# Attention with a gated squared-ReLU branch on one core: key, value and output-weight loads split, and two output rows moved to other buffers

## The chip, the cores and the metric

The kernel runs on one core of one Trainium2 chip, as one launch. The core has five engines that each run their own list of instructions in order: TensorE (PE) for matmuls, VectorE (DVE), ScalarE (ACT), GpSimd (POOL) and SyncE (SP), which here only issues transfers. They meet through semaphores. The metric is the device time of one execution in microseconds; the time before is the median of five.

## The reference

A layer norm of x (2048 rows of 512) feeds two branches: attention over a given cache of keys and values (32 heads, 2048 keys, head size 128) and a dense branch with a squared ReLU. The output is x plus their product, the dense branch passed through silu.

```
xn = _layernorm(x)
q  = (xn @ wq) per head                       # wq: 512 x 4096
p  = softmax(q @ k_cache^T * 128 ** -0.5)
s  = concat over heads of (p @ v_cache) @ wo  # wo: 4096 x 512
h  = xn @ w1 + b1                             # w1: 512 x 1792
g  = silu(relu(h) ** 2 @ w2 + b2)
return x + s * g
```

All inputs and the output are bfloat16.

## The kernel before

The 2048 rows are cut into NQB = 4 blocks of 512 query rows. A block goes through all 32 heads, so there are NG = 128 heads of work, numbered g = 0 to 127. The 2048 keys of a head are taken 256 at a time: NPR = 8 steps a head, 1024 steps (`pi`) in all. In a step `gen_scores` (lines 658 to 691) makes two matmuls of 512 columns into PSUM (`psA`, two halves in turn), and one ACTIVATE on ACT takes the exp of 128 x 1024 scores into one of NPT = 8 buffers of `pT`. Two steps later (LAG = 2) the probabilities meet the values.

That second product has two forms. In form A (`gen_pv`, line 952) the probabilities are the stationary operand, and a column of ones beside the values gives the softmax's denominator: 64 matmuls of 129 columns a head. DVE then copies the result to `o_un`, divides it, and a DMA transpose on SP's queue brings it into `oT`. In form B (`gen_pv_b`, line 713) the values are stationary: 16 matmuls of 512 columns a head, and the result comes out already transposed (`o_col`). The denominator must then be made apart: POOL adds the two halves of a step's probabilities into `h_sum` (`part_add`, line 745) and DVE reduces that into `d_part` (`part_half`, 753), or DVE does both alone (`den_part`, 732). `den_sum`, `den_write`, `den_read`, `den_total`, `den_recip`, `den_spread` and `den_scale` (lines 764 to 810) bring the sums together by way of a small DRAM tensor, `d_scr`, spread the reciprocals into `r_all`, and POOL scales `o_col` into `oT`. A `pT` buffer is free again only when the value matmuls and the denominator's reads of it are done; the exp eight steps later waits for that.

Which form a head takes, and in which order everything stands on each engine, is settled while the program is built. The class `_Sched` keeps a clock for each engine, from the rough costs in `_cost` (line 60) and, for DMAs on SP, the pairs (issue, landing) in `_ISSUE` (line 97). `choose` takes form B unless the first or last three heads are at hand or `owed`, the planned backlog of DVE, is 9000 ns or more. Denominator work waits in lists (`quiet`, `pool_quiet`, `sync_quiet`) and is put between other instructions where that clock has room (`fill_dve`, `fill_pool`, `fill_sync`, lines 892 to 946). So an edit that changes an entry of `_ISSUE`, or adds an instruction to SP, can change the order on all engines.

Beside attention TensorE has jobs (`job_proj`, `job_h`, `job_o2`, `job_wo`, lines 1048 to 1186) that `fill_one` puts between the steps: the projection of the queries two heads ahead, the dense branch, and the output product in groups of eight heads. The output product's parts are summed in `acc`; `acc_gate` (line 1194) multiplies `acc` by the gate on DVE, `acc_add` (1201) adds x on POOL, and the last part is multiplied by the gate into `tmp_t`, added to `acc` and written out. Row tiles, 128 rows each, are numbered jt = 0 to 15. Their results stand in `out_t`, which has two buffers used in turn, but for the very last, jt = 15, which goes to `x_t`.

Transfers into SBUF are almost all issued by SP, in order. `kT` and `v_sb` have NSL = 3 slots, one a head. In step k = 0 of head g the loop issues `fill_wq(g + 3)` and `fill_k(g + 2)` (a DMA transpose of the head's 2048 x 128 keys), and in step 1 `fill_v(g + 2)` (512 KB). A key load waits for the last score of the head that used the slot, a value load for its last value product. The output weights come in four loads of 1 MB at steps 60, 84, 108 and 132. Between these stand `den_write` and `den_read`, the `oT` transposes, and in the opening the loads of w1 and w2.

Of the kernel before, what the change touches and what calls it, by code (L numbers as in the profile page):

```python
# [10 lines left out]
P = 128  # L11
# [73 lines left out]
def _uses_port(name, fn):  # L85
# [3 lines left out]
    if name == "DVE":  # L89
        if f in (_tt, _stt):  # L90
            return _in_sbuf(k["in0"]) and _in_sbuf(k["in1"])
        if f in (_ts, _copy):
# [1 line left out]
    return False  # L94


_ISSUE = {"kT": (2450, 4900), "oT": (1230, 3400), "xnT": (1230, 3400), "v_sb": (450, 4750),
          "wo_all": (1700, 7200), "w1_sb": (600, 5000), "w2_sb": (700, 5000), "d_scr": (530, 2200),
          "d_quad": (1230, 4200)}


# [199 lines left out]
def bass_recurrent_scan__mha_block_cached__dense_activation_squared_relu__prompt_kernel(  # L301
# [14 lines left out]
    _, H, Sk, Dh = A_k_cache.shape  # L316
# [3 lines left out]
    NQB = Sq // QB  # L320
    TPB = QB // P
    NDC = D // P
    NKT = Sk // P
    NPR = NKT // 2
# [6 lines left out]
    HC = 8  # L331
    NCH = H // HC
    CH = [[(m * HC, (m + 1) * HC) for m in range(NCH)] for _ in range(NQB - 1)]
    CH.append([(0, HC), (HC, 2 * HC), (2 * HC, H)])
    LAG = 2
    ROOM = 800
    LATE = 150
    LATE_EVICT = 250
# [6 lines left out]
    S = _Sched()  # L345
# [4 lines left out]
    SP = S.eng("SP")  # L350
# [9 lines left out]
    xnT = sb("xnT", [P, NDC, 2 * QB], BF16)  # L360
    w1_sb = sb("w1_sb", [P, NDC, F], BF16)
    w2_sb = sb("w2_sb", [P, NFC, D], BF16)
    wo_all = sb("wo_all", [P, H, D], BF16)
    h2T = sb("h2T", [P, NFC, QB], BF16)
    g_all = sb("g_all", [P, TPB, D], BF16)
    oT = sb("oT", [P, NOT, QB], BF16)
    acc = sb("acc", [P, TPB, D], F32)
    kT = sb("kT", [P, NSL, Sk], BF16)
    v_sb = sb("v_sb", [P, NSL, NKT, VW], BF16)
# [14 lines left out]
    d_scr = nc.dram_tensor("d_scr", [2, 32, 4 * NBK], F32, kind="Internal").ap()  # L384
# [25 lines left out]
    def bankF(i):  # L410
        return psF[:, i * 512:(i + 1) * 512]
# [4 lines left out]
    sl_k = [S.slot(f"k{i}") for i in range(NSL)]  # L416
    sl_v = [S.slot(f"v{i}") for i in range(NSL)]
# [9 lines left out]
    sl_wo = [S.slot(f"wo{i}") for i in range(NCH)]  # L427
# [94 lines left out]
    t_kT0 = [None, None]  # L522
# [88 lines left out]
    t_kfill = [None] * NG  # L611
    t_vfill = [None] * NG
    t_wqfill = [None] * NG
    t_S_last = [None] * NG
    t_PV_last = [None] * NG
# [8 lines left out]
    t_wodone = {}  # L624
    wo_view = A_wo.rearrange("(h p) d -> p h d", p=P)

    def fill_k(g):
        if g >= NG:
            return
        h, i, prev = g % H, g % NSL, g - NSL  # L630
        t_kfill[g] = S.emit_dma(SP, partial(_dmaT, out=kT[:, i, :], in_=A_k_cache[0, h, :, :]),
                                sl_k[i], deps=[t_S_last[prev] if prev >= 0 else t_kT0[1]])

    def fill_v(g, eng=SP):
        if g >= NG:
            return
        h, i, prev = g % H, g % NSL, g - NSL
        t_vfill[g] = S.emit_dma(
            eng, partial(_dma, out=v_sb[:, i, :, 0:Dh],
                        in_=A_v_cache[0, h].rearrange("(t p) d -> p t d", p=P)), sl_v[i],  # L640
            deps=[t_PV_last[prev] if prev >= 0 else None])

    def fill_wq(g, eng=SP):
        if g >= NG:
# [4 lines left out]
                        in_=A_wq[:, h * Dh:(h + 1) * Dh].rearrange("(c p) e -> p c e", p=P)),  # L649
            sl_wq[i], deps=[t_proj[prev] if prev >= 0 else None])  # L650

    def load_wo(i):
        tok_wo[i] = S.emit_dma(
            SP, partial(_dma, out=wo_all[:, i * HC:(i + 1) * HC, :],
                        in_=wo_view[:, i * HC:(i + 1) * HC, :]), sl_wo[i])


    def gen_scores(pi):
# [161 lines left out]
    def calm(due, fn):  # L820
        quiet.append((due, fn if isinstance(fn, partial) else partial(fn)))
# [130 lines left out]
    def gen_pv(pi):  # L952
# [40 lines left out]
        if last:  # L993
            t_PV_last[g] = t
            m = a_no[g]
            for b in range(2):
# [3 lines left out]
                    deps=[t_bank[b], t_norm[m - 1] if m else None], late=LATE_EVICT)  # L1000
            calm(pi + LAG + 3, partial(norm_recip, g))
            pool_quiet.append(partial(norm_scale, g))
# [42 lines left out]
    def at(step, fn):  # L1045
        events.setdefault(step, []).append(fn)
# [86 lines left out]
    def job_wo(j, m, qt, c0=0, c1=D):  # L1133
        jt = j * TPB + qt
        h0, h1 = CH[j][m]
        nh = h1 - h0
        last = m == len(CH[j]) - 1
        box = [None]

        def mm(n, bank):  # L1140
            g = j * H + h0 + n
            assert tok_oT[g] is not None
            place, free = (bankF(bank), t_bankF[bank]) if isinstance(bank, int) else bank
            box[0] = E(PE, partial(_mm, out=place[:, 0:c1 - c0],
                                   lhsT=oT[:, g % NOT, qt * P:(qt + 1) * P],
                                   rhs=wo_all[:, h0 + n, c0:c1], start=(n == 0),
                                   stop=(n == nh - 1)),
                       deps=[tok_wo[(h0 + n) // HC], tok_oT[g], free], inc=(n == nh - 1))

        def evac(bank, step):  # L1150
            if qt == TPB - 1:
                for h in range(h0, h1):
                    t_wodone[j * H + h] = box[0]
            place = (bankF(bank) if isinstance(bank, int) else bank[0])[:, 0:c1 - c0]
            if m == 0:
                t_acc[qt] = t = E(DV, partial(_copy, out=acc[:, qt, :], in_=place),
                                  deps=[box[0], t_fin.get(jt - TPB)])
            elif not last:
                t_acc[qt] = t = E(DV, partial(_tt, out=acc[:, qt, :], in0=place,
                                              in1=acc[:, qt, :], op=ALU.add),  # L1160
                                  deps=[box[0], t_acc[qt]])
            if m == len(CH[j]) - 2:
                calm(step + 16, partial(acc_gate, j, qt))
                pool_quiet.append(partial(acc_add, j, qt))
            if last:
                s = jt % 2
                assert all(x in t_g for x in t_o2j)
                t = E(DV, partial(_stt, out=tmp_t[:, s, c0:c1], in0=place, scalar=0.5,
                                  in1=g_all[:, jt % TPB, c0:c1], op0=ALU.mult,
                                  op1=ALU.mult),  # L1170
                      deps=[box[0], t_g[jt], t_tmp[s], t_zrd[s]])
                end = jt == NQB * TPB - 1
                row = (x_t if end else out_t)[:, s, c0:c1]
                eng = GP if j == NQB - 1 and qt in (0, 2) else DV
                t_fin[jt] = t_tmp[s] = E(
                    eng, partial(_tt, out=row, in0=tmp_t[:, s, c0:c1],
                                 in1=acc[:, qt, c0:c1], op=ALU.add),
                    deps=[t, t_u[jt], None if end else t_outdma[s]])
                eng, sl = (SP, sl_fin) if j == NQB - 1 else (GP, sl_out)
                dma = S.emit_dma(  # L1180
                    eng, partial(_dma, out=out[0, jt * P:(jt + 1) * P, c0:c1],
                                 in_=row), sl[s], deps=[t_fin[jt]])
                if c1 == D:
                    t_outdma[s] = dma
            return t
        return nh, mm, evac
# [23 lines left out]
    for j in range(NQB):  # L1210
        b = 30 + j * (SPB - 6)
        for c in range(NFC):
            k = b + (SPB * 9 // 256) * c
            jobs.append((k, max(k - 130, 4), job_h(j, c), (None, j)))
        for qt in range(TPB):
            k = b + (SPB * 9 // 256) * NFC + (SPB * 28 // 256) * qt
# [113 lines left out]
    for i in range(NFC // 2):  # L1330
        at(40 + 2 * i, partial(load_w2, i))
    for i in range(NCH):
        at(60 + 24 * i, partial(load_wo, i))
    for j in range(NQB):
        if j + 1 < NQB:
            for i in range(TPB):
# [69 lines left out]
    end = NPAIR  # L1406
    backfill[0] = fill_dve
    for pi in range(NPAIR):
        g, k = divmod(pi, NPR)
        if k == 0 and g > 0:  # L1410
            m = len(b_heads)
            choose(g, FIRST_B <= g < NG - 3 and owed(pi) < OWED and (m < NOC or m - NOC in t_dr))
            if is_b(g):
                plan_b(g)
        if pi >= NPR:
            gen_scores(pi)
        credit = 1.0 if pi < NPR else min(credit + left[0] / max(end - pi, 1), 8.0)
        n = 0
        most = 0 if pi < NPR else 3 if k == 2 else 2
        while n < most:  # L1420
            late = any(isinstance(p, int) and NPR * p <= pi + 12
                       for p in [cur_proj[0]] + [x[3] for x in jobs[:4]])
            if not (credit >= 1.0 or late):
                break
            if k == 1 and cur[0] is not None and cur[0][1] == cur[0][0][0] - 1:
                break
            if not fill_one(pi) and not (not jobs and tail_one(pi)):
                break
            credit = max(credit - 1.0, 0.0)
            left[0] -= 1  # L1430
            n += 1
        if pi >= NPR:
            gen_pv(pi - LAG)
        if k == 0:
            fill_wq(g + 3)
            fill_k(g + 2)
        if k == LAG - 1:
            fill_v(g + 2)
        pending.extend(events.pop(pi, []))
        if k >= 2:  # L1440
            for fn in [pending.pop(0) for _ in range(min(2, len(pending)))]:
                fn()
        fill_all(ROOM)
    for pi in range(NPAIR - LAG, NPAIR):
        gen_pv(pi)
    while quiet or pool_quiet or sync_quiet:
        n = len(quiet) + len(pool_quiet) + len(sync_quiet)
        fill_all(ROOM, flush=True)
        assert len(quiet) + len(pool_quiet) + len(sync_quiet) < n
# [42 lines left out]
```

## Time and profile before

| | us |
|---|---|
| median of 5 runs (1220.05 to 1220.60) | 1220.38 |
| the profiled execution, its own time | 1220.05 |
| its span, first instruction to last | 1218.3 |
| ACT busy: 1025 exps of 128 x 1024, 1.024 each | 1036.7 of 1088.5 |
| POOL busy: 764 additions into `h_sum`, 1.163 each | 867.0 of 1067.4 |
| DVE busy: 764 reductions of `h_sum`, 0.686 each | 506.3 of 1077.5 |
| key transposes from the second head on: 127, median to landing | 4.6 |
| value loads of 512 KB: 127, median to landing | 4.4 |

Busy time is the union of an engine's instructions. A matmul of 512 columns is shown with 0.379 us, but matmuls overlap in the array, so that their starts lie closer together. PE is the matmuls, PEld the weight loads that run beside them. A line of the timeline or of the groups names the engine, the helper's line, the operation, what it writes and reads, the shapes and the count; in square brackets stands how long the engine was idle before it, and who ended that.

### The profile page before, as it was taken

To read this page: it belongs to the slowest core of one execution; us is meant where nothing else is said; L and a number is where in the kernel's file an instruction comes from. 1 tells how busy PE (TensorE), PEld (TensorE's weight loads), DVE (VectorE), ACT (ScalarE), POOL (GpSimd) and SP (SyncE) were. 2 spreads that over 40 slices of the span, in tenths; PEclk is the share of its full clock that TensorE was granted. 3 is DMA by queue.
4 is the path that set the end of the run, shared out by engine and by line. 5 is a ranking of instruction groups with operands and counts; after the bars stand their busy time and mean duration, and the time that the engine had idled before them with its cause. 6 is when DMAs were issued, how large, how long until landed. Compare 5 with 4: busy or idle time off the path is not lost.

```text
span 1218.3 us, 19228 instructions
## 1 busy us (share of the span) xinstructions
PE 1206.2 (99%) x6386; PEld 588.4 (48%) x6509; DVE 1077.5 (88%) x1820; ACT 1088.5 (89%) x1157; POOL 1067.4 (88%) x978
## 2 busy tenths in 40 slices
PE   9999999999999999999999999999999999999998
PEld 7544444445454454444554444444444544444455
DVE  4798999898989888999999989898999899889983
ACT  7898999998988989999899899998989999989994
POOL 1799999998978989999888899999989789899981
PEclk9999999999999999999999999999999999999999
DMA  9998886667777776766687677766776687667651
GB/s 226 201 228 173 178 172 126 132 135 140 138 153 147 138 137 129 141 136 127 138 146 166 133 136 142 140 127 130 142 141 132 132 157 135 129 131 146 130 119 31
DMA packets 655492, 174.83 MB, mean 144 GB/s; under 512 B 642176, under 2 KB 654208, under 8 KB 655392
## 3 DMA queue, kind: packets, MB, share of 16 engines
q1 hardware_dynamic: 653296, 169.52, 70.1%
q0 software_dynamic: 1424, 3.81, 1.1%
q8 instruction: 52, 0.85, 0.3%
q14 instruction: 48, 0.39, 0.1%
q10 hardware_dynamic: 672, 0.26, 0.1%
HBM read 100.27 MB, written 3.01 MB: 85 GB/s over the span
## 4 chain that ended last, share of the span: by engine, by line
PE 94%; DVE 3%; POOL 1%; issue 1%; ACT 0%; ACTq 0%; POOLq 0%; DVEq 0%
PE psA L226 35%; PE psO L226 30%; PE psF L226 24%; PE psO L231 4%; DVE d_part L286 1%; POOL h_sum L239 1%; DVE acc L249 0%; ACT pT L235 0%; PE psA L231 0%; DVE h2T L249 0%; DVE r_t L245 0%; POOL oT L239 0%; DVE r_all L290 0%; DVE qt_sb L253 0%; DVE x_t L239 0%
## 5 line engine op out<-in xcount | busy, mean ns | idle before, releaser
L235 ACT ACTIVATE pT<-psA 128x1024 bf16<-128x1024 f32 x1025 | 1036.7, 1024 | 110.6 <-PE psA L226 70.6
L239 POOL TENSOR_TENSOR h_sum<-pT 128x512 f32<-128x512 bf16 x764 | 867.0, 1163 | 35.8 <-ACT pT L235 15.0
L226 PE MATMUL psA<-qt_sb,kT 128*128 128x512 bf16 x1976 | 592.3, 379 | 4.1 <-ACT pT L235 1.1
L286 DVE TRANSPOSE_TENSOR_REDUCE d_part<-h_sum 128x16 f32<-128x512 f32 x764 | 506.3, 686 | 31.8 <-POOL h_sum L239 29.3
L226 PE MATMUL psO<-pT,v_sb 128*128 128x512 bf16 x1759 | 525.9, 379 | 1.9
L226 PEld LDWEIGHTS psA<-qt_sb,kT 128*128 128x128 bf16 x2032 | 193.5, 98 | 213.2 <-ACT pT L235 4.4
L226 PEld LDWEIGHTS psO<-pT,v_sb 128*128 128x128 bf16 x1792 | 175.3, 98 | 211.5 <-issue 1.2
L239 POOL TENSOR_TENSOR oT<-o_col,r_all 128x512 bf16<-128x512 f32 x112 | 144.6, 1292 | 30.7 <-DVE r_all L290 30.4
L226 PE MATMUL psF<-xnT,wq_sb 128*128 128x512 bf16 (+1 forms) x511 | 166.5, 374 | 0.6 <-DVE xnT L253 0.2
L286 DVE TRANSPOSE_TENSOR_REDUCE d_part<-pT 128x32 f32<-128x1024 bf16 x132 | 159.2, 1213 | 4.5 <-ACT pT L235 4.1
L226 PE MATMUL psF<-wo_all,oT 128*128 128x512 bf16 x468 | 160.1, 379 | 0.7
L253 DVE CAST qt_sb<-psF 128x512 bf16<-128x512 f32 (+1 forms) x130 | 87.0, 670 | 23.2 <-PE psF L226 20.3
L231 PEld LDWEIGHTS psO<-v_sb,pT 128*128 128x128 bf16 x1024 | 68.1, 98 | 28.8 <-ACT pT L235 0.4
L226 PEld LDWEIGHTS psF<-xnT,wq_sb 128*128 128x128 bf16 x520 | 50.3, 98 | 60.0 <-issue 0.3
L231 PE MATMUL psO<-v_sb,pT 128*128 128x129 bf16 x1024 | 78.6, 220 | 0.2
L290 DVE STREAM_TRANSPOSE r_all<-d_rec 128x512 f32<-128x512 f32 x112 | 76.8, 686 | 0.5
L226 PE MATMUL psF<-xnT,w_sb 128*128 128x512 bf16 x216 | 74.7, 379 | 0.2
L226 PEld LDWEIGHTS psF<-wo_all,oT 128*128 128x128 bf16 x480 | 46.9, 98 | 56.4
L226 PE MATMUL psF<-w_sb,h2T 128*128 128x512 bf16 x219 | 72.4, 379 | 0.2
L235 ACT ACTIVATE o_col<-psO 128x512 f32<-128x512 f32 x112 | 66.3, 592 | 0.0
L245 DVE TENSOR_SCALAR r_t<-psF,b1f 128x512 bf16<-128x512 f32 x56 | 41.1, 734 | 15.5 <-PE psF L226 14.0
L282 DVE TENSOR_REDUCE d_sum<-d_part 128x16 f32<-128x144 f32 (+3 forms) x112 | 43.1, 385 | 1.1
(60 smaller groups left out, 405.0 us busy)
## 6 DMA issues: line engine op xcount, KB each, us to landing
v_sb<-in_A_v_cache_dram SPq DMA_DIRECT2D x127, 512.0 KB, 4.4
wq_sb<-in_A_wq_dram SPq DMA_DIRECT2D x127, 128.0 KB, 2.5
wo_all<-in_A_wo_dram SPq DMA_DIRECT2D x4, 1024.0 KB, 6.4
w_sb<-in_B_w_dram SPq DMA_DIRECT2D x14, 256.0 KB, 4.3
d_quad<-d_scr SPq DMA_DIRECT2D x112, 32.0 KB
x_t<-in_A_x_dram POOLq DMA_DIRECT2D x16, 128.0 KB, 3.7
kT<-in_A_k_cache_dram SPq DMA_TRANSPOSE x127, 4.6
x_ln<-in_A_x_dram SPq DMA_DIRECT2D x15, 128.0 KB, 3.5
```

Source lines behind the costliest of these rows:

```text
L226: return e.matmul(out, lhsT, rhs, start=start, stop=stop)
L231: return e.matmul(out, lhsT, rhs, start=start, stop=stop, skip_group_check=True)
L235: return e.activation(out, in_, func, bias=bias, scale=scale)
L239: return e.tensor_tensor(out, in0, in1, op)
L245: return e.tensor_scalar(out, in0, scalar1=scalar1, scalar2=scalar2, op0=op0, op1=op1)
L253: return e.tensor_copy(out, in_)
L282: return e.tensor_reduce(out, in_, axis=AX.X, op=ALU.add)
L286: return e.tensor_reduce(out, in_, axis=AX.X, op=ALU.add, apply_transpose=True)
L290: return e.transpose(out, in_)
```

## The change

The keys of a head are loaded in NKP = 2 transposes of 1024 keys, at steps 0 and 4; the values in NVP = 4 loads of 128 KB, at steps 1, 3, 5 and 7; each chunk of output weights in NWP = 4 loads of 256 KB, six steps apart. All parts of a slot raise one semaphore, and whoever reads the slot waits for the last of them. Where `fill_k` and `fill_v` are called without a part (head 1, at the start), all parts are issued one after another. The planner's costs in `_ISSUE` for `kT`, `v_sb` and `wo_all` are set for the new sizes. And the last two row tiles, jt = 14 and 15, both go to `x_t`, where only jt = 15 did.

```diff
-_ISSUE = {"kT": (2450, 4900), "oT": (1230, 3400), "xnT": (1230, 3400), "v_sb": (450, 4750),
-          "wo_all": (1700, 7200), "w1_sb": (600, 5000), "w2_sb": (700, 5000), "d_scr": (530, 2200),
+_ISSUE = {"kT": (1230, 3400), "oT": (1230, 3400), "xnT": (1230, 3400), "v_sb": (450, 3000),
+          "wo_all": (600, 4000), "w1_sb": (600, 5000), "w2_sb": (700, 5000), "d_scr": (530, 2200),
           "d_quad": (1230, 4200)}
...
+    NKP, NVP, NWP = 2, 4, 4
...
-    def fill_k(g):
+    def fill_k(g, part=None):
         if g >= NG:
             return
         h, i, prev = g % H, g % NSL, g - NSL
-        t_kfill[g] = S.emit_dma(SP, partial(_dmaT, out=kT[:, i, :], in_=A_k_cache[0, h, :, :]),
-                                sl_k[i], deps=[t_S_last[prev] if prev >= 0 else t_kT0[1]])
-
-    def fill_v(g, eng=SP):
+        n = Sk // NKP
+        for x in range(NKP) if part is None else [part]:
+            t_kfill[g] = S.emit_dma(
+                SP, partial(_dmaT, out=kT[:, i, x * n:(x + 1) * n],
+                            in_=A_k_cache[0, h, x * n:(x + 1) * n, :]),
+                sl_k[i], deps=[t_S_last[prev] if prev >= 0 else t_kT0[1]],
+                group_done=x == NKP - 1)
+
+    def fill_v(g, part=None):
         if g >= NG:
             return
         h, i, prev = g % H, g % NSL, g - NSL
-        t_vfill[g] = S.emit_dma(
-            eng, partial(_dma, out=v_sb[:, i, :, 0:Dh],
-                        in_=A_v_cache[0, h].rearrange("(t p) d -> p t d", p=P)), sl_v[i],
-            deps=[t_PV_last[prev] if prev >= 0 else None])
+        n = NKT // NVP
+        for x in range(NVP) if part is None else [part]:
+            t_vfill[g] = S.emit_dma(
+                SP, partial(_dma, out=v_sb[:, i, x * n:(x + 1) * n, 0:Dh],
+                            in_=A_v_cache[0, h].rearrange("(t p) d -> p t d",
+                                                          p=P)[:, x * n:(x + 1) * n, :]),
+                sl_v[i], deps=[t_PV_last[prev] if prev >= 0 else None],
+                group_done=x == NVP - 1)
...
-    def load_wo(i):
+    def load_wo(i, x):
+        n = HC // NWP
+        h0 = i * HC + x * n
         tok_wo[i] = S.emit_dma(
-            SP, partial(_dma, out=wo_all[:, i * HC:(i + 1) * HC, :],
-                        in_=wo_view[:, i * HC:(i + 1) * HC, :]), sl_wo[i])
+            SP, partial(_dma, out=wo_all[:, h0:h0 + n, :], in_=wo_view[:, h0:h0 + n, :]),
+            sl_wo[i], group_done=x == NWP - 1)
...
-                end = jt == NQB * TPB - 1
+                end = jt >= NQB * TPB - 2
                 row = (x_t if end else out_t)[:, s, c0:c1]
...
     for i in range(NCH):
-        at(60 + 24 * i, partial(load_wo, i))
+        for x in range(NWP):
+            at(60 + 24 * i + 6 * x, partial(load_wo, i, x))
...
         if k == 0:
             fill_wq(g + 3)
-            fill_k(g + 2)
-        if k == LAG - 1:
-            fill_v(g + 2)
+        if k % (NPR // NKP) == 0:
+            fill_k(g + 2, k * NKP // NPR)
+        if k % (NPR // NVP) == LAG - 1:
+            fill_v(g + 2, k * NVP // NPR)
```

## The prediction

> **What bounds the kernel now.** I read the page first (busy shares, chain), then the waits, then the timeline around the few waits that reach TensorE.
>
> ```profile
> span 1218.3 us, 19228 instructions
> PE 1206.2 (99%) x6386; PEld 588.4 (48%) x6509; DVE 1077.5 (88%) x1820; ACT 1088.5 (89%) x1157; POOL 1067.4 (88%) x978
> ...
> DMA  9998886667777776766687677766776687667651
> ...
> PE 94%; DVE 3%; POOL 1%; issue 1%; ACT 0%; ACTq 0%; POOLq 0%; DVEq 0%
> ```
>
> The reader is to see that TensorE is busy 99% of the span and carries 94% of the chain that ends last, and that the DMA engines are full only in the first slices. A busy share can hide slow matmuls, so I priced the work itself. In the timeline a run of 17 matmuls of 512 columns takes 3.83 us from first start to last end, the last one 0.379 us long: (3.83 - 0.379) / 16 = 0.216 us apart. Twelve of 129 columns take 0.84 us, the last 0.22: 0.0565 us apart. The program has 5272 matmuls of 512 columns (2032 scores, 1792 values, 504 query projections, 448 of the dense part, 496 output) and 1024 of 129: 5272 x 0.216 = 1138.8, 1024 x 0.0565 = 57.9, and small ones 14.6, together 1211.3 us. Of 1218.3 only about 7 are left: 1.0 before the first matmul, 3.1 after the last one ends (1215.2), and 2.9 of gaps. Between 17 us and 1200 us the only gap of size is this one:
>
> ```profile
> 904.17 0.62 PE L231 MATMUL psO<-v_sb,pT 128*128 128x129 bf16 x8
> 905.85 0.60 PE L226 MATMUL psA<-qt_sb,kT 128*128 128x512 bf16 x2 [1.06 <-ACT pT L235]
> ...
> ```
>
> ```profile
> 904.77 4.06 ACT L235 ACTIVATE pT<-psA 128x1024 bf16<-128x1024 f32 x4 [1.87 <-POOL h_sum L239]
> ```
>
> ```profile
> 891.72 3.08 DVE L249 SCALAR_TENSOR_TENSOR acc<-acc,g_all 128x512 f32<-128x512 f32 x1
> ...
> 897.48 2.30 DVE L249 SCALAR_TENSOR_TENSOR acc<-acc,g_all 128x512 f32<-128x512 f32 x1
> ```
>
> Scores wait for an exp, the exp for POOL to finish reading the probabilities' buffer, and POOL was late because two gates of `acc` on DVE took 3.08 and 2.30 us (the shortest take 0.65 to 0.75) beside POOL's additions. The weight loads waited 1.24 us for it. No wait of a compute engine on a key, value or weight transfer stands in the list of waits; the only DMA waits there are for `x_ln` at the start (3.5 us) and for a row's output in the tail.
>
> **The change part by part.** *Smaller transfers.* Per head SP issued one key transpose (median 1.863 us) and one value load (0.379). Now it issues two transposes and four loads. A half transpose isn't in the trace; it lies between the smaller `oT` transpose (1.228) and the full one (1.863), so two cost 2.46 to 3.73; I take 2.8, nearer the small one. Four value loads: 4 x 0.379 = 1.52. With one wq load (0.48) and the denominator's write and read (0.53, 0.55), SP goes from 3.8 to 5.9 us a head (6.8 at most) of 1218.3 / 128 = 9.5. SP computes nothing; what hides this is the distance from issue to use. A step is 1218.3 / 1024 = 1.19 us. The second key half is issued at step 4 of head g for head g+2, 12 steps before its first score: 14.3 less 4.6 (median landing) leaves 9.7 us. The last value quarter goes at step 7, 11 steps before use: 13.1 less 4.4 leaves 8.7. Before, the plan left 16 steps (14.4) and 17 (15.8); the trace's smallest distance from landing to use after the opening was 10.06 and 10.14 us (head 76), so SP ran late by up to 4.3 and 5.7. The same lateness leaves 5.4 and 3.0 us: nothing on the path. Without that cover each further us of SP lateness is one of TensorE. Behind SP's waits for `d_sum` (longest 5.2 us) and for the landing in `d_scr` (3.3) now stand fewer bytes at a time. The 16 loads of 256 KB for wo are out by step 78 for the first chunk, used from step 88: 11.9 us against 4.3 us for a `w_sb` load of the same size. Cost 0.
>
> *The opening* is where cover is thinnest:
>
> ```profile
> 13.38 2.74 SPq L298 DMA_TRANSPOSE kT<-in_A_k_cache_dram  x1
> 16.17 0.58 SPq L294 DMA_DIRECT2D v_sb<-in_A_v_cache_dram  x1
> 16.80 3.23 SPq L294 DMA_DIRECT2D w_sb<-in_B_w_dram  x2
> 20.07 0.51 SPq L294 DMA_DIRECT2D wq_sb<-in_A_wq_dram  x1
> ```
>
> Head 2's keys landed at 19.9 and were used at 26.2; head 4's wq landed at 23.8 and was used at 26.7, the tightest. In the new order head 2's second key half stands behind two w1 loads and two value quarters, and eight more issues (3 + 3 value loads, 2 halves) precede that wq. By 23.8 us the DMAs had moved 4992 KB, 222 GB/s, with the engines full (share 1.01 in the first 100 us); issues were held back (a w1 issue of 2.5 us against 0.58). So bytes set the landings, and the same bytes precede the wq: 23.8 again, and 384 KB earlier, 22.0, for the key half. Lower bound 0; upper bound all eight issues added at 0.5 each, 27.8 against 26.7: 1.1 us. I take 0.1, since the engines are full.
>
> The Trainium skill's page "DMA: Bandwidth & Descriptors", section "Bandwidth", speaks against this: batch to 1 MiB or more, with about 2.0 us fixed per transfer and bytes over 436 GB/s (measured for loads issued by GpSimd). Taken one after another, an estimate by it is 4 x 2.3 + 2 x 2.6 + 2.3 = 16.7 us of loads a head against 9.5, over 900 us more. The trace's own pair of 256 KB value loads, issued at 3.58 and 4.12, took 4.9 and 5.3 us to land, so they overlap.
>
> *The planner's figures.* New issue times shift its clock for SP, and with it the order on all engines: one head changes from the 129-column form to the 512-column form (113 such heads, not 112). TensorE: 64 x 0.0565 = 3.62 out, 16 x 0.216 = 3.46 in: **-0.16 us**. The head adds 0.59 us to ACT and some 7 us to POOL (six additions of 1.163 and a scaling of 1.292 for one of 1.040), hidden by their idle 11 to 12%. The gates of `acc`, counted by query evictions on DVE, stood before at heads 95, 96 and 97, two within 6 us; now at 94, 97 and 98. With more room I take the wait at 905 as gone: **-1.24** (bounds 0 and -1.24). What new waits the order makes can't be read from it: from 0 to one such wait at each of three block ends and one in the opening, 4 x 1.24 = 4.96. I take **+0.5**, by the row of 17 to 871 us, where weight loads waited for exps 0.7 us in all.
>
> *Row buffers.* The tail before:
>
> ```profile
> 1213.31 1.27 POOL L239 TENSOR_TENSOR out_t<-z_t,acc 128x512 bf16<-128x512 f32 x1 [1.92 <-DMA out_dram<-out_t]
> ```
>
> ```profile
> 1213.93 0.93 DVE L239 TENSOR_TENSOR x_t<-z_t,acc 128x256 bf16<-128x256 f32 x1
> 1214.96 0.29 DVE L249 SCALAR_TENSOR_TENSOR z_t<-psA,g_all 128x128 f32<-128x128 f32 x1
> ```
>
> POOL's addition for row tile 14 waited 1.92 us for tile 12's output to leave `out_t`. It ran until 1214.58, and DVE's addition of 256 columns beside it took 0.93 us; by 0.29 for 128 columns and 0.736 for 512 it should take 0.44. With its own buffer POOL starts when the product is ready, 1212.54 + 0.09, and ends at 1213.90, just before DVE's addition at 1213.93. DVE then catches up with TensorE, whose last matmul ends at 1215.22: last product 1215.26, last addition ends 1215.87 and not 1216.30: **-0.43** (bound 0, if the two still meet).
>
> *Sum.* Span 1218.30 - 0.16 - 1.24 - 0.43 + 0.1 + 0.5 = 1217.07. The profiled execution took 1220.05, 1.75 more than its span, and lies 0.33 under the median: 1217.07 + 1.75 + 0.33 = 1219.15, so **1219.1**.
>
> **The rivals.** (1) The wait at 905 stays or moves: for it speaks that the same work meets near head 95; against it the wider spacing. 1220.38 - 0.16 - 0.43 = 1219.8. (2) The opening starves: 1219.1 + 1.0 = 1220.1; against it the full DMA engines. (3) The other side: the new order delays POOL, which holds probabilities' buffers, at four places as at 905, one mechanism. For it speaks one head of relief fewer for POOL and DVE; against it that 17 to 871 us shows 0.7 us. It costs 4.96: 1220.38 - 0.16 - 1.24 - 0.43 + 4.96 = 1223.5; it decides from the fourth such wait. (4) The transfers were hidden and stay so, and more is gained than I see: of TensorE's 2.9 us of gaps 2.9 - 1.24 = 1.7 lie mostly in the first 17 us, and losing 1.5 of them gives 1217.6. Against it: those early loads keep their order. That the smaller transfers do nothing by themselves is part of the forecast: its gain comes from the order and the tail.
>
> **How the numbers follow.** Forecast 0.47, (1) 0.22, (2) 0.06, (3) 0.18, (4) 0.07. A change within 0.2%, 2.4 us, can't be told from none here: 1217.9 to 1222.8. Forecast, (1) and (2) lie in it: 0.75; slower 0.18; faster 0.07. The range runs from 1217.9, past the forecast without the 0.6 of assumed waits (1218.5), to 1222.4, the forecast with three waits as at 905 in place of half of one (1219.1 + 3.2).
>
> **What would show it.** Right: TensorE's waits after 17 us below 1 us, no wait on `kT`, `v_sb` or `wo_all`, DVE's 256-column addition near 0.44 us, POOL's last addition without its 1.92 us wait. Wrong: score weight loads waiting for `pT` with POOL behind it at several places, or waiting for a transfer near 26 us; a half transpose that takes SP as long as a whole one.

## The result, and the profile after

| | us |
|---|---|
| median after (27 runs, 1220.66 to 1223.22) | 1222.44 |
| median before, same chip (47 runs, 1219.83 to 1221.95) | 1220.11 |
| ratio after to before, 95% interval | 1.0016 [1.0011, 1.0022] |
| the profiled execution of after, its own time | 1223.14 |
| its span | 1221.3 |

The changed kernel is 2.3 us slower: inside the 0.2% of the prediction, but its interval lies wholly on the slow side, and 1222.44 is above the range (1217.9 to 1222.4) and 3.3 us above the forecast of 1219.1. It also varies more: 2.6 us from its fastest run to its slowest.

The page of after, its span, busy times and chain (each engine with its busy microseconds, share and instruction count):

```profile
span 1221.3 us, 19712 instructions
...
PE 1207.1 (99%) x6339; PEld 586.6 (48%) x6461; DVE 1084.7 (89%) x1829; ACT 1089.4 (89%) x1158; POOL 1074.3 (88%) x986
...
PE 92%; DVE 3%; POOL 2%; issue 1%; DMA 1%; ACT 0%; ACTq 0%; POOLq 0%
```

TensorE is still what ends last, but its part of the chain fell from 94% to 92%; POOL has 2% where it had 1%, and a DMA, absent before, stands there with 1%. The busy row hides the loss (99% both times). The list of waits shows it (engine and what it was about to do, whom it waited for: microseconds in total, times, longest):

```profile
PE psA L226 <- ACT pT L235: 2.0, 2, 1.1
...
PE psF L226 <- DVE h2T L249: 0.7, 1, 0.7
PE psO L226 <- DVE o_un L253: 0.6, 1, 0.6
...
DVE d_rec L282 <- DMA d_quad<-d_scr: 2.3, 1, 2.3
```

Two things are new. TensorE has five gaps where the kernel before had one of size (four of them are in this list), and VectorE waits for `d_quad`, the read of the denominators: no compute engine waited for such a transfer before. Measured between weight loads, as in the prediction, TensorE's new gaps are 1.08 us at 73, 0.48 at 98, 1.12 at 100, 1.34 at 105 and 0.91 at 314 us: 4.93 in all. The old gap of 1.24 us at 905 is gone. With the 0.16 of the one head in the shorter form, 4.93 - 1.24 - 0.16 = 3.5 us up to the end of the last matmul; measured 3.17 (1215.22 to 1218.39), so some 0.4 us less went into gaps too small to list. Behind it the engines end 0.42 us sooner than before, but the last output's transfer then takes 2.30 us to the end of the span where it took 1.96, so that only 0.1 us of the tail's gain is left in this execution.

*The opening.* The first head's denominators in the timeline of the kernel before (start, length, what is issued or done):

```profile
50.66 0.68 SPq L294 DMA_DIRECT2D d_scr<-d_sum  x1
53.29 0.56 SPq L294 DMA_DIRECT2D d_quad<-d_scr  x1
```

```profile
58.82 0.25 DVE L282 TENSOR_REDUCE d_rec<-d_quad 128x16 f32<-128x64 f32 x1
```

SyncE's queue in the timeline of after:

```profile
48.35 2.48 SPq L298 DMA_TRANSPOSE kT<-in_A_k_cache_dram  x1
...
52.05 0.51 SPq L294 DMA_DIRECT2D v_sb<-in_A_v_cache_dram  x1
52.60 1.43 SPq L298 DMA_TRANSPOSE kT<-in_A_k_cache_dram  x1
54.07 0.69 SPq L294 DMA_DIRECT2D d_scr<-d_sum  x1
54.81 1.50 SPq L294 DMA_DIRECT2D v_sb<-in_A_v_cache_dram  x2
59.10 0.57 SPq L294 DMA_DIRECT2D d_quad<-d_scr  x1
```

And what VectorE and then POOL did there (in brackets the idle time before, and who ended it):

```profile
61.40 0.26 DVE L282 TENSOR_REDUCE d_rec<-d_quad 128x16 f32<-128x64 f32 x1 [2.33 <-DMA d_quad<-d_scr]
...
62.43 1.15 POOL L239 TENSOR_TENSOR h_sum<-pT 128x512 f32<-128x512 bf16 x1 [3.01 <-DVE d_rec L257]
```

The first head of form B has its sums ready at 50.56 us (50.40 before). Before, their write was issued at 50.66 and the read at 53.29, and VectorE used the result at 58.82 without a wait. After, SyncE is still issuing parts of keys and values at 50.56; the write goes out at 54.07, the read at 59.10, and VectorE, which works in order, stands still for 2.33 us with POOL behind it for 3.01.

Late issue is only part of this. The write is issued 3.4 us later than before, the read 5.8. From 56.31 to 59.10 SyncE issues nothing: it waits for the write to land, and the read follows the write by 5.03 us where it was 2.63. SyncE's own list of waits has this as its longest of the kind:

```profile
SPq L294 <- DMA d_scr<-d_sum: 11.6, 16, 2.8
```

So the parts ahead make the small write go out later and land more slowly; no run here takes the two apart.

*The order.* Timeline of after at block 1's first row, on three engines:

```profile
98.86 3.63 DVE L245 TENSOR_SCALAR xn_t<-x_ln,mv_t,rstd 128x512 bf16<-128x512 bf16 x1
...
98.98 3.36 POOL L239 TENSOR_TENSOR h_sum<-pT 128x512 f32<-128x512 bf16 x3
...
101.31 0.61 PE L226 MATMUL psA<-qt_sb,kT 128*128 128x512 bf16 x2 [0.91 <-ACT pT L235]
```

The same `xn_t` in the kernel before:

```profile
92.90 0.99 DVE L245 TENSOR_SCALAR xn_t<-x_ln,mv_t,rstd 128x512 bf16<-128x512 bf16 x1
```

It took 0.99 us there. Here it lasts as long as POOL's three additions beside it; VectorE's reductions of `h_sum` come late, POOL's next addition too, and scores wait for an exp that waits for POOL.

*The tail* did on the engines what was forecast (timeline of after, POOL's last addition and VectorE's of 256 columns):

```profile
1215.78 1.26 POOL L239 TENSOR_TENSOR x_t<-z_t,acc 128x512 bf16<-128x512 f32 x1 [1.23 <-DVE z_t L249]
...
1217.10 0.42 DVE L239 TENSOR_TENSOR x_t<-z_t,acc 128x256 bf16<-128x256 f32 x1
```

POOL waits for its operand `z_t` alone, no longer for an output to leave, and the 256 columns take 0.42 us where they took 0.93.

### The profile page after: what moved, and what is told of

It reads as the page before. It is cut to its first block, busy times and chain, and to the rows that moved or that the text cites. A ratio compares the mean times of both kernels' runs of the same rounds, so it can differ in the third digit from the quotient of the medians.

```text
span 1221.3 us, 19712 instructions
## 1 busy us (share of the span) xinstructions
PE 1207.1 (99%) x6339; PEld 586.6 (48%) x6461; DVE 1084.7 (89%) x1829; ACT 1089.4 (89%) x1158; POOL 1074.3 (88%) x986
## 4 chain that ended last, share of the span: by engine, by line
PE 92%; DVE 3%; POOL 2%; issue 1%; DMA 1%; ACT 0%; ACTq 0%; POOLq 0%
PE psA L226 34%; PE psO L226 30%; PE psF L226 24%; PE psO L231 4%; POOL h_sum L239 2%; DVE d_part L286 1%; ACT pT L235 0%; DMA d_scr<-d_sum 0%; DVE r_t L245 0%; POOL oT L239 0%; DVE acc L249 0%; PE psA L231 0%; DVE h2T L249 0%; DVE r_all L290 0%; DMA d_quad<-d_scr 0%
## 5 line engine op out<-in xcount | busy, mean ns | idle before, releaser
L235 ACT ACTIVATE pT<-psA 128x1024 bf16<-128x1024 f32 x1025 | 1037.1, 1024 | 112.5 <-PE psA L226 72.8
L286 DVE TRANSPOSE_TENSOR_REDUCE d_part<-h_sum 128x16 f32<-128x512 f32 x772 | 512.8, 685 | 33.1 <-POOL h_sum L239 30.4
L231 PEld LDWEIGHTS psO<-v_sb,pT 128*128 128x128 bf16 x960 | 63.8, 98 | 26.8 <-ACT pT L235 0.4
L231 PE MATMUL psO<-v_sb,pT 128*128 128x129 bf16 x960 | 73.7, 220 | 0.1
```

What stands on the lines that cost most here:

```text
L231: return e.matmul(out, lhsT, rhs, start=start, stop=stop, skip_group_check=True)
L235: return e.activation(out, in_, func, bias=bias, scale=scale)
L286: return e.tensor_reduce(out, in_, axis=AX.X, op=ALU.add, apply_transpose=True)
```

## The experiments

From the start there were two theories. Theory Q: the parts fill SyncE's queue, and the denominator's small write and read come late in it. Theory O: the planner's new order on the engines makes new waits. To part them, the split was separated from the planner: a part with `clock` false goes into SyncE's queue but the planner's clock doesn't see it, and where `whole` is true the first part loads everything and the others nothing. A kernel in "the old order" so has PE, ACT, DVE and POOL exactly as in the kernel before (the later parts of the output weights then take no turn in the planner's list of events), and one in "the new order" as in the changed kernel. Ratios are to the kernel before on the same chip; its median was 1220.05 for the first four kernels, 1220.07, 1220.22 and 1220.01 for the later groups.

**The parts of the change, one at a time.** Split transfers in the old order, old row buffers (e1_parts_old_order; against the changed kernel, with `_ISSUE` and `end` as before):

```diff
-                group_done=x == NKP - 1)
+                group_done=x == NKP - 1, real=x == 0 or not whole, clock=x == 0)
...
-                group_done=x == NVP - 1)
+                group_done=x == NVP - 1, real=x == 0 or not whole, clock=x == 0)
```

> The split transfers at their new steps, but planned at the old costs, so that TensorE, ACT, DVE and POOL have exactly the order of the kernel before; old row buffers. Theory Q (SP's queue: in the opening the first denominators' write and read stand behind key and value parts, DVE waits for them at about 59 us and stays late until about 105 us): slower than before by 2 to 4 us, 1222 to 1224, with a DVE wait for d_quad near 59 us and score weight loads waiting before 110 us; the wait at 905 us stays. Theory O (the planner's new order itself makes the waits): 1220.1, as before.

Measured: 1221.23 us (1220.10 to 1222.76), ratio 1.0009 [1.0000, 1.0018]. The parts alone cost 1.2 us at the median, with an interval that just reaches no change, and in the fastest execution nothing: that is the profiled one, 1220.1, and no engine waits for a denominator in it.

The new order with whole transfers and old row buffers (e2_new_order_whole): `_ISSUE` as changed, `whole = True` and `clock=True` everywhere.

> The reverse: TensorE, ACT and DVE in exactly the order of the changed kernel, but each key, value and output-weight chunk moved whole, at its first part's place; old row buffers. Q: no DVE wait for d_quad, no waits of score weight loads before 110 us, the wait at 905 us gone, that at 314 us (0.9 us) kept: 1220.1 - 0.16 - 1.24 + 0.9 = 1219.6. O: about as the changed kernel, 1222.4.

Measured: 1221.29 us (1220.99 to 1222.47), ratio 1.0010 [1.0001, 1.0019]. The order alone costs 1.2 us; nine of the eleven runs lie within 0.4 us of each other, two above 1222. Its profile accounts for it: gaps of 0.36 us at 99, 1.34 at 103 and 0.91 at 312 us, less the 1.24 at 905 and the 0.16 of the shorter head, make +1.2. The long `xn_t` is there too (timeline of this run):

```profile
96.67 3.58 DVE L248 TENSOR_SCALAR xn_t<-x_ln,mv_t,rstd 128x512 bf16<-128x512 bf16 x1
...
96.72 3.37 POOL L242 TENSOR_TENSOR h_sum<-pT 128x512 f32<-128x512 bf16 x3
```

Keys and values split from head 16 on only, output weights whole, old order (e3_split_from_head16):

```diff
-            whole = not 0 <= g < 1000000000
+            whole = not 16 <= g < 1000000000
```

> Old order, old row buffers; keys and values split only from head 16 on, output weights whole. Q: the opening is as before, so 1220.1 within 0.4. If the parts cost something in every head (more issues on SP all along): above 1221. O: 1220.1.

Measured: 1220.86 us (1219.98 to 1225.23), ratio 1.0011 [1.0002, 1.0019]. Neither nothing nor all: five of eleven runs lie within 0.5 us of the kernel before, three above 1223. The profiled execution took 1220.4; in it VectorE waits once, 1.0 us, for `d_quad` at 169 us, some 30 us after the parts set in, and no TensorE gap follows. So the opening isn't the only place where a denominator can be late; the three above 1223 weren't profiled.

The row buffers alone, in the old order with whole transfers (e4_rows_only):

```diff
-                end = jt == NQB * TPB - 1
+                end = jt >= NQB * TPB - 2
```

> The kernel before with row tiles 14 and 15 both in the x buffers, nothing else. The prediction's step gives -0.43: 1219.7. The changed kernel's trace, where the time from the last matmul's start to the end of the span is 3.17 us and not 3.26, gives -0.1: 1220.0. In the profile DVE's addition of 256 columns takes 0.42 us in both cases.

Measured: 1219.68 us (1219.31 to 1219.80), ratio 0.9995 [0.9987, 1.0004]: 0.37 us less than before. The interval takes in no change; the size agrees with the 0.43 worked out from the tail's lines, and here the last output's transfer takes 1.95 us as before.

Order +1.24, parts +1.18, rows -0.37 make 1220.11 + 2.05 = 1222.2; measured 1222.44.

**What in the order costs.** The new order, whole transfers, and POOL's addition into `h_sum` that started beside `xn_t` held back until `xn_t` is done (e5_order_hold; `writes` lists the places in an engine's program that write a tile):

```diff
+    for name, which, add in [('xn_t', 4, 42)]:
+        at_dve = writes(DV, name)[which]
+        done = sum(u is not None for w, fn, u in DV.prog[:at_dve + 1])
+        GP.prog[writes(GP, "h_sum")[add]][0].append((DV.sem, done))
```

> The order of the changed kernel with the old whole transfers and old row buffers (the run before at 1221.29 us), and one wait more: GpSimd's addition into h_sum that started at 96.7 us there, the first of three in a row, waits until VectorE's xn_t of block 1's first row is done. That xn_t took 3.6 us beside the three additions and 0.99 us in the kernel before. Theory O1 (the waits of 0.36 and 1.34 us for exp at 98 to 103 us come from that one long VectorE instruction): they go, and the time falls by about 1.7 us to 1219.6. Theory O2 (exp is late for another reason, the additions on GpSimd themselves come late): holding GpSimd back by about 1 us more makes the waits longer, 1221.3 to 1222.5.

Measured: 1220.56 us (1220.26 to 1221.27), 0.73 less than without the wait. `xn_t` now takes 0.38 us (timeline of this run):

```profile
97.06 0.38 DVE L248 TENSOR_SCALAR xn_t<-x_ln,mv_t,rstd 128x512 bf16<-128x512 bf16 x1
...
97.58 4.47 POOL L242 TENSOR_TENSOR h_sum<-pT 128x512 f32<-128x512 bf16 x4 [0.33 <-DVE xn_t L248]
```

Both theories hold in part: of the two waits of 0.36 and 1.34 us one of 1.14 is left, behind POOL's four additions, now in a row. So holding POOL back gave back 0.73 of the order's net 1.24 us. That the rest is work on POOL which the order has placed too tightly is a reading of the trace, not shown by a run.

The same means for the kernel before, with the row buffers (e6_before_hold_rows): the additions beside the two gates of `acc` at 892 and 897 us wait for them, `[('acc', 9, 575), ('acc', 10, 578)]`.

> The kernel before in its own order, with the last two row tiles in buffers of their own (1219.68 us alone), and two waits more: GpSimd's additions into h_sum that ran beside VectorE's gate products at 891.7 and 897.5 us wait until these are done. Theory O1 (the wait of 1.24 us at 905 us is made by gates that last 2 to 3 us beside GpSimd's additions and 0.7 us alone): the wait goes, 1219.68 - 1.24 = 1218.4 us, below both kernels. Theory O2 (the chain up to 905 us is set by GpSimd's own additions): the time stays at 1219.7 or rises.

Measured: 1218.72 us (1218.44 to 1219.08), ratio 0.9988 [0.9979, 0.9997]: faster than both kernels. The gates in the timeline of this run, and the scores that waited 1.06 us before:

```profile
891.76 0.84 DVE L252 SCALAR_TENSOR_TENSOR acc<-acc,g_all 128x512 f32<-128x512 f32 x1
...
896.51 0.65 DVE L252 SCALAR_TENSOR_TENSOR acc<-acc,g_all 128x512 f32<-128x512 f32 x1
...
904.87 0.61 PE L229 MATMUL psA<-qt_sb,kT 128*128 128x512 bf16 x2
```

The gates take 0.84 and 0.65 us where they took 3.08 and 2.30, and the gap at 905 falls from 1.24 to 0.27 us. What this brings without the rows, 0.96 us, fits that. That chain, which the prediction only argued, is now shown for the gap at 905: it was the lengthening of VectorE's instructions beside POOL's.

**What in the parts costs.** Split transfers in the old order as in e1, and on SyncE's queue the denominator's write and read of the first 8 heads of form B moved ahead of up to five parts (e7_parts_den_first):

```diff
+    left, at_sp = 2 * 8, 0
+    while left and at_sp < len(SP.prog):
+        if tile(SP.prog[at_sp]) in ("d_scr", "d_quad"):
+            to = at_sp
+            while at_sp - to < 5 and tile(SP.prog[to - 1]) in ("kT", "v_sb", "w1_sb", "w2_sb"):
+                to -= 1
+            SP.prog.insert(to, SP.prog.pop(at_sp))
+            left -= 1
+        at_sp += 1
```

> The split transfers in the old order of the engines (1221.23 us, 1220.1 to 1222.8, before), and on SyncE's queue the denominator's write and read of the first 8 heads of the second form moved ahead of up to five parts. Theory Q1 (the cost of the parts is that these two small transfers stand behind more issues in the opening, up to 110 us): 1220.1 to 1220.4 us, and little spread. Theory Q2 (the parts delay them everywhere, or they move through the 16 queues' memory at the expense of something else all along the span): stays near 1221.2 with its spread.

Measured: 1220.02 us (1219.74 to 1220.47), ratio 0.9998 [0.9989, 1.0007]. The whole cost is gone, and the spread with it, by moving 15 small transfers (the sixteenth had no part just ahead of it), each past one to five parts; every part is still there. Timeline of this run:

```profile
50.45 0.68 SPq L297 DMA_DIRECT2D d_scr<-d_sum  x1
...
53.02 0.58 SPq L297 DMA_DIRECT2D d_quad<-d_scr  x1
...
58.84 0.25 DVE L285 TENSOR_REDUCE d_rec<-d_quad 128x16 f32<-128x64 f32 x1
```

Write, read and use are back within 0.3 us of where they were before the change. The read again follows the write by 2.6 us, so that this run removes the late issue and the slow landing together. With the parts and without the lateness the time is that of the kernel before: in the old order the parts cost nothing else.

Only the values split, old order (e8_values_split): `whole` false for `v_sb` alone. Only the keys (e9_keys_split): for `kT` alone.

> The old order of the engines, old row buffers; only the values are loaded in four parts over a head's steps, keys and output weights whole. Theory Q1 or Q2 where the number of issues counts (values bring 381 of the 556 new issues): most of the +1.2 us, 1220.8 to 1221.2. If it is the keys' halves (1.2 us of issue each, twice a head at new places): no cost, 1220.0 to 1220.3.

> The old order of the engines, old row buffers; only the keys are loaded in two halves over a head's steps, values and output weights whole. Values alone cost all of it (1221.42 us, 1220.13 to 1223.37). Theory K0 (a half takes SyncE half as long to issue, 1.2 us beside 2.4 us, so no small transfer stands behind more work): 1220.0 to 1220.2 us with a spread under 1 us. Theory K1 (any part more in the queue costs): 1220.5 to 1221.

Measured: values 1221.42 us (1220.13 to 1223.37), ratio 1.0009 [1.0000, 1.0018]; keys 1220.31 us (1220.12 to 1224.01), ratio 1.0003 [0.9994, 1.0012]. It is the values in the main. (The split brings 520 new issues, 381 + 127 + 12, of which 381 are the values'; e8's expectation says 556.) In the profile of e8 the way from the late read to TensorE can be followed in three lines of the timeline:

```profile
91.94 0.26 DVE L285 TENSOR_REDUCE d_rec<-d_quad 128x16 f32<-128x64 f32 x1 [1.32 <-DMA d_quad<-d_scr]
...
94.55 1.27 POOL L242 TENSOR_TENSOR oT<-o_col,r_all 128x512 bf16<-128x512 f32 x1 [2.80 <-DVE r_all L293]
...
96.45 0.59 PE L229 MATMUL psO<-pT,v_sb 128*128 128x512 bf16 x2 [1.44 <-DVE o_un L256]
```

VectorE waits 1.32 us; everything in its list moves back, among it the copy `o_un` that empties the bank `psO`; the value matmuls wait for that bank. The keys' halves make VectorE wait for `d_quad` as well, three times for 2.4 us in all, but no wait of TensorE followed in the profiled run; two of its eleven timed runs were above 1222.

The values in four parts issued back to back at the old step (e10_values_back_to_back):

```diff
-        if k % (NPR // NVP) == LAG - 1:
-            fill_v(g + 2, k * NVP // NPR)
+        if k == LAG - 1:
+            fill_v(g + 2)
```

> The old order; the values in four parts of 128 KB as in the run of the values alone, but all four issued one after the other at the step at which the whole was issued. The number of issues is the same (381 more), only their places in SyncE's queue are the old ones. Theory P (the place: parts late in a head's steps stand just ahead of the denominator's write and read): 1220.0 to 1220.4 us. Theory C (the count: SyncE has some 1.5 us more to issue for each head wherever they stand, and in the opening it has no idle time for it): 1221.0 to 1221.8 us, as spread as the values alone.

Measured: 1222.57 us (1221.33 to 1225.84), ratio 1.0018 [1.0010, 1.0027]: worse than the parts spread over the steps. So it isn't the late place in a head's steps; spreading softens the cost. The profiled execution, at 1225.6 well above the median, has these waits for `d_quad`, and this line in its timeline:

```profile
DVE d_rec L285 <- DMA d_quad<-d_scr: 4.9, 4, 2.8
```

```profile
98.68 0.59 PE L229 MATMUL psO<-pT,v_sb 128*128 128x512 bf16 x2 [1.85 <-DVE o_un L256]
```

**The changed kernel mended.** With the denominators of the first 8 heads moved ahead as in e7 (e11_after_den_first), with those of all heads (e12_after_all_den_first, `2 * 400` in place of `2 * 8`), and with the values alone loaded whole (e13_after_values_whole, `whole = True` for `v_sb`):

> The changed kernel (1222.44 us), every engine in its own order but SyncE, where the denominator's write and read of the first 8 heads of the second form are moved ahead of up to five parts. Theory: the three parts of the change add up (order +1.24, split transfers +1.2 of which all is these 16 small transfers, rows -0.37), so 1220.05 + 1.24 - 0.37 = 1220.9 us. Rival: in the new order the waits for exp come out of the late denominators too, then 1219.7 to 1220.2; or the two don't add up and it stays above 1221.8.

> As the run before it, but the denominator's write and read of all 112 heads of the second form are moved ahead of up to five parts. Theory: only the opening decides (a later head has 8 us and more from the sum to the use): 1220.9 us again. Rival: late heads cost too, as the parts from head 16 on alone did (1220.86 us, up to 1225): 1220.3 us or less, with less spread. If SyncE, now waiting for each sum ahead of the parts, makes the keys late: above 1221.5 us.

> The changed kernel with every engine's order its own, keys in halves and output weights in quarters as changed, row buffers as changed; only the values are loaded whole, at step 1. Theory V (the values' parts are all that the transfers cost, in the new order too): the new order with whole transfers, 1221.29 us, less 0.37 for the rows = 1220.9 us, with a spread under 1 us, and no wait of VectorE for d_quad in the opening. Rival (in the new order keys and output weights cost too, by late denominators): 1221.5 us or more.

Measured: 1221.63 us (1221.14 to 1222.16), 1222.08 (1221.36 to 1222.99) and 1220.86 (1220.54 to 1222.31); ratios 1.0006 [0.9997, 1.0015], 1.0013 [1.0004, 1.0022] and 1.0008 [0.9999, 1.0017]. The last is what the sum gave (1220.9): in the new order too, all that the transfers cost comes from the values' parts, though VectorE still waits 0.63 us for the first `d_quad` in its profile, which the expectation excluded. Moving the denominators ahead gave back only 0.8 and 0.4 of the 1.5 us there. The profile of e11 shows one reason: the first head's 2.33 us are gone, but VectorE waits 1.42 us for the `d_quad` of a head whose sums end at 60.2. The edit moves a transfer past parts alone and stops at any other, and this read stood behind a load of wq, so it still went out only at 68.84. That late denominators are the whole of the values' cost is thus shown in the old order; in the changed kernel they are shown for about half of it, and why moving all of them is no better stays open.

**How the cost goes with the count.** Values in two parts and in eight, old order (e14_values_two_parts, e15_values_eight_parts): `NVP` 2 and 8, for eight with two parts at each of the four steps.

> The old order, keys and output weights whole, values in two parts of 256 KB at steps 1 and 5: 127 more issues than before instead of 381. Theory N (the cost goes with the number of issues): a third of 1.35 us, 1220.5 us. Theory T (a threshold: it costs once the write of the sums is pushed past the slack of the opening's first heads): 1220.0 to 1220.2 us.

> The old order, keys and output weights whole, values in eight parts of 64 KB, two at each of the steps 1, 3, 5 and 7: 889 more issues than before instead of 381. Theory N: SyncE's issues go up by 4 x 0.5 us a head more; in proportion 1220.05 + 1.35 x 889 / 381 = 1223.2 us; as delays in a chain that is late already count in full, it may be above 1224. If the number of bytes in flight, not the number of issues, makes the small transfers late: no more than with four parts, 1221.0 to 1221.8 us.

Measured: 1219.96 us (1219.81 to 1220.14), ratio 1.0000 [0.9991, 1.0009], and 1236.05 us (four runs, 1233.38 to 1236.88), ratio 1.0127 [1.0113, 1.0141]. Not in proportion: two parts cost nothing, four 1.35 us, eight 16 us. With eight, VectorE's waits for `d_quad` are (list of waits of e15):

```profile
DVE d_rec L285 <- DMA d_quad<-d_scr: 18.8, 11, 7.5
...
PEld psF L229 <- DMA wq_sb<-in_A_wq_dram: 2.9, 2, 1.7
```

The second line is new in kind: at 27 and 59 us TensorE itself waits for a load of wq from the same queue. So not all of the 16 us is the denominators'.

Set side by side, with SyncE's issue time added up between 50 and 100 us of each profile:

| values in | SyncE busy, 50 to 100 us | VectorE's waits for `d_quad` | median |
|---|---|---|---|
| one load (before) | 69% | none | 1220.1 |
| two parts | 71% | none | 1219.96 |
| four parts | 88% | 2.5 us, 2 times | 1221.42 |
| four parts, back to back | 86% | 4.9 us, 4 times | 1222.57 |
| eight parts | 93% | 18.8 us, 11 times | 1236.05 |
| all of e7, denominators first | 88% | 0.2 us, once | 1220.02 |

Each row's share and waits are those of one profiled execution, and the share is rough: e4 and e6, with whole loads issued as in the kernel before, show 77% and 76%. They and e2, e5 also show `d_quad` waits of 0.5 to 0.8 us with whole loads, so that a wait of this size need not cost anything. The last row says that the busy queue isn't the cost in itself: with 88% and the small transfers ahead there is none. The cost sets in where a round trip at whose end VectorE stands no longer fits.

## Why the prediction was wrong

- *"Smaller transfers", cost 0: wrong, and the first step that failed.* What it worked out of the keys, values and weights held: no wait for `kT`, `v_sb` or `wo_all` stands in the list, halves landed in 3.2 us and quarters in 2.5 (issue rows below). But the distance from issue to use was checked for those three alone. The two transfers behind them in the same queue, `d_scr` and `d_quad`, got one sentence ("now stand fewer bytes at a time"), and they had the least slack: a write, a landing, a read and a landing in 8.4 us in the opening, 50.40 to 58.82. The load was taken as a mean over a head, 5.9 us of 9.5, where in the opening the first write now stood behind more issues, landed more slowly, and the read came 5.8 us later. Measured: +1.18 us in the old order (e1), 1.48 in the new, (1222.44 - 1220.11) - (1220.86 - 1220.01). The prediction's estimate of over 900 us for loads taken one after another did not come: in e7 all the parts together cost nothing. (The fixed 2.0 us in it stands in the section "Anatomy of one DMA — SWDGE (gpsimd) path" of the page that the prediction names, not in "Bandwidth".)

```profile
v_sb<-in_A_v_cache_dram SPq DMA_DIRECT2D x508, 128.0 KB, 2.5
...
wo_all<-in_A_wo_dram SPq DMA_DIRECT2D x16, 256.0 KB, 3.1
kT<-in_A_k_cache_dram SPq DMA_TRANSPOSE x254, 3.2
```

- *"What new waits the order makes … I take +0.5": mis-sized, the largest error.* The step named the mechanism and its bounds (0 to 4.96) and took a value near the low end from the quiet stretch of 17 to 871 us. Measured in e2: 0.36 + 1.34 + 0.91 = 2.6 us. With -1.24 and -0.16 the order gives +1.2 and not -0.9. That stretch was quiet in the old order; it said nothing about another order of the same work. (The head in the other form also brought eight additions to POOL, 772 against 764, and not six; no run prices that.)
- *The wait at 905 us, -1.24: right*, and for the reason given: the gates of `acc` stand at 888, 909 and 919 us in after, no longer two within 6 us.
- *Row buffers, -0.43: right* (-0.37 alone, e4); in the profile of after a slower last transfer takes back most of it.
- *The opening, +0.1*: its stated mechanism, wq and key loads late at 26 us, didn't occur in the changed kernel (it did with eight parts, e15, where a wait for wq ends at 27.6 us); the opening lost its time later, to the denominators. The gaps at 73 and 98 us of after aren't in the profile of e13, where the values are whole.
- *Rivals.* Number 3, new waits behind POOL at four places, came half: TensorE waits for exps behind POOL at 100 and 105 us, 2.46 us together, and at three other places for VectorE. It had 0.18, and nothing in it was the transfers' doing. A rival in which the parts delay another transfer of the same queue was missing.

From the forecast's change of -1.2 us to the measured +2.3: the order accounts for 2.1 us (from -0.90 to +1.24), the parts for 1.1 (from +0.10 to +1.18), the rows for 0.1; 0.3 is left over, less than the runs' own scatter. The executions' spread, which the forecast didn't speak of, comes mostly from the parts: the order alone varies by 1.5 us, the values alone by 3.2, and by 0.7 with the denominators ahead (e7).

## What to carry to other kernels

When transfers are cut into more issues, price the other transfers of that queue: take the one with the shortest way from ready to use, list what is now issued ahead of it at its busiest stretch, and compare that with its slack there, not with a mean. If it doesn't fit, move the small, urgent transfers ahead: in the old order that recovered all that the parts had cost, in the changed kernel about half at best. And a change of a planner's costs is a new order of all engines, whose price has to be looked for around each place where two engines lengthen each other's work; a wait there can be ended by holding back a few instructions, as the 1218.72 us of the old order with three small edits shows.

## What the runs showed of the hardware

A smaller value load wasn't issued faster: on SyncE a whole one of 512 KB took 0.38 us (median), a quarter 0.49, an eighth 0.47. A key transpose took 1.86 and its half 1.22, so two halves take longer than the whole. The Trainium skill's page "DMA: Bandwidth & Descriptors", section "Issuing engines are not separate DMA queues", calls the sequencer's time to start a DMA usually small relative to the DMA itself. That holds here for a quarter of the values, 0.49 us against 2.5 to landing, less so for a key half, 1.22 against 3.2. Yet added up ahead of an urgent write this time put it off by 3.4 us in the opening, and its slower landing took another 2.4.

One VectorE instruction of 128 x 512 bf16 took 0.38 us with POOL held back, 0.99 in the kernel before and 3.6 beside three POOL additions in a row, ending 0.15 us after the last of them. The Trainium skill's page "SBUF — State Buffer", section "SBUF: two separate sides", describes an exclusive lock between certain VectorE operations and GpSimd's, held for a whole instruction. The trace shows the times and not the lock; they agree in kind, but here VectorE's instruction lasted through three of POOL's and not one.
